# Attention followed by a gated MLP on one core: the third group's softmax denominators summed on GpSimd in float32

## The chip, the cores and the metric

One core of a Trainium2 chip runs the whole program. The metric is the device time of one execution in microseconds (us), the median of several runs; lower is better. The engines are named as in the profile: PE (TensorE, the matmul array; PEld is its weight load), DVE (VectorE), ACT (ScalarE), POOL (GpSimd) and SP (SyncE, which issues transfers here).

## What is computed

Eight batches, twelve heads, 448 tokens, head dimension 64. Queries and keys are normalised by their root mean square, attention is taken in each head, and its output goes, token by token, through a layer of 768 to 2048 with a leaky gate and a layer back to 768.

```python
def rmsnorm(x, g):
    rms = np.sqrt(np.mean(x * x, axis=-1, keepdims=True) + 1e-06)
    return x / rms * g
q_n, k_n = (rmsnorm(q, g_q), rmsnorm(k, g_k))
scores = np.matmul(q_n, k_n.transpose(0, 1, 3, 2)) / np.sqrt(64)
scores = scores - np.max(scores, axis=-1, keepdims=True)
attn = np.exp(scores)
attn = attn / (np.sum(attn, axis=-1, keepdims=True) + 1e-09)
x = np.matmul(attn, v)        # then heads side by side: 3584 x 768
h = x @ w_in                  # 768 -> 2048
g = np.maximum(h, 0.0) + alpha * np.minimum(h, 0.0)
out = g @ w_out               # 2048 -> 768
```

The denominators of the softmax, `np.sum(attn)` over the keys, are what the change is about. The kernel uses a fixed bias in the exponential in place of the maximum.

## The kernel before

**Tiles.** A batch has three *groups* of four heads; `y` counts groups over all batches, 0 to 23, so y = 2, 5, 8, ... is the third group of a batch. The 128 partitions hold two heads at a time (g = 0 and 1, 64 partitions each), and `par` = 0 and 1 are the other two. The 448 keys are cut into J = 7 chunks of 64.

**Attention of a group.** `score(y, j)` makes the scores of one chunk of keys against all queries in PSUM (tile sc, L323); `soft(y, j)` takes the exponential on ACT (L337) into `expT[y][:, j]`, 128 partitions by 2 x 448 in float16, with the keys of the chunk on the partitions. `den(ys)` sums over keys by products with a tile of ones, so that the denominators come out repeated over partitions (tile dn, L352 by way of `over_keys`); `attv(ys, half)` does the same walk with the values as weights (tiles av and avb). `over_keys` has 28 or 56 small products for a group: m = 64 columns of weights up to group 8, m = 32 from group 9 on (EARLY = 9), 64 rows each, so that four or eight of them use separate parts of the array. The loop over chunks j is the outermost, and each part accumulates over j. `log` (L369) and `invert` (L374) make 1/denominator on ACT as exp(-ln d), and a product on DVE (L403, L401) writes the normalised output into `xT`.

The first two groups of a batch are treated as a pair: one `den` for both. The third group stands alone, with a `den` of its own.

**MLP.** `up(b, ft)` is a *gate group*: six products of 128x448 into one PSUM bank (hT or hTa, L418), the scaled copy ah on ACT (L458), the maximum on DVE (L462) into gT. `down(b0, t, oh)` is a *down group*: sixteen products of 128x384 (op or opa, L472), a copy on DVE (L484), and two stores issued on SP.

**PSUM.** Pool pss has two buffers of two banks for scores. Pool psf has two single banks with tag "mm", shared by the gate groups hT, the down groups op, and avb. Pool psa has one buffer of two banks with tag "acc": dn and av, and now and then a gate or down group, then called hTa or opa (the flag `spare`).

**Normalisation of q and k.** For each group: load (SP), square on POOL (L152), sum on DVE (L160), root on ACT (L170, L171), scaling on POOL (L176), transposition by a transfer from group 7 on, the gain on DVE (L285).

**Order.** All engines' queues are written out by hand in program order; nothing reorders them. The unit is the *burst* n, 69 in all: two to four scores and exponentials, with a `den` or an `attv` between them where `dens[n]` or `avs[n]` says so, and behind them `gaps[n]`, a list of gate and down groups of an earlier batch. A planner fills the gaps: `cost(n)` estimates a burst's own TensorE time, UP = 1.13 and DOWN = 2.6 that of the groups, and each burst gets work until its share of the period is spent. `prep`, `post`, `roots` and `jobs` hang the loads, squares, roots and sums of later groups on bursts, counted back from `den_at` and `av_at`. In the last part, after burst 68, `rest` holds the last batch's MLP.

For a third group, the `den` stands in one burst and the `attv` in the next, each between scores:

```python
if n in dens and not lead:
    den(dens[n])
if n in avs and not lead:
    for half in (1, 0) if avs[n] == (0, 1) else (0,):
        attv(avs[n], half)
```

Of the kernel before, what the change touches and what calls it, by code (L numbers as in the profile page):

```python
# [21 lines left out]
def kernel(  # L22
# [26 lines left out]
    TD = min(7, NG)  # L49
    EB = 3  # L50
    EARLY = 3 * G
    assert G == 3

    cst = ctx.enter_context(tc.tile_pool(name="cst", bufs=1))
# [19 lines left out]
    nc.vector.memset(epsb, RMS_EPS)  # L74
    ones = cst.tile([128, 64], FP16, name="ones", tag="ones")
    nc.vector.memset(ones, 1.0)
    ident = cst.tile([128, 128], FP16, name="ident", tag="ident")
    make_identity(nc, ident)
    ident32 = cst.tile([32, 32], FP32, name="ident32", tag="ident32")
# [233 lines left out]

    expT, rden, scs = {}, {}, {}

    def score(y, j):
        qT, kT = qkT[y, "q"], qkT[y, "k"]
        sc = pss.tile([128, 2, 512], FP32, name="sc", tag="sc")
        m = 64 if y < EARLY else 32
        for c in range(64 // m):  # L320
            for par in range(2):
                for g in range(2):
                    nc.tensor.matmul(  # L323
                        out=sc[ds(64 * g + m * c, m), par, :S].rearrange(
                            "p (j c) -> p j c", j=J
                        ),
                        lhsT=kT[ds(64 * par, 64), j, g, ts(c, m)],
                        rhs=qT[ds(64 * par, 64), :, g, :],
                        start=True,
                        stop=True,  # L330
                    )
        scs[y, j] = sc

    def soft(y, j):
# [4 lines left out]
            scale=QK_SCALE, bias=expb[:, 0:1],  # L339
        )  # L340

    def over_keys(accs, ys, weights):

        m = 64 if len(ys) == 1 and ys[0] < EARLY else 32
        if len(ys) == 2:
            heads = [(y, par, 0) for y in ys for par in range(2)]
        else:
            heads = [(ys[0], par, c) for par in range(2) for c in range(64 // m)]
        for j in range(J):
            for h, (y, par, c) in enumerate(heads):  # L350
                for g in range(2):
                    nc.tensor.matmul(  # L352
                        out=accs[g][ds(m * h, m), :S],
                        lhsT=weights(g, y, par, ts(c, m), j),
                        rhs=expT[y][ds(64 * g, 64), j, par, :],
                        start=(j == 0),
                        stop=(j == J - 1),
                    )

    def den(ys):  # L360
        dn = psa.tile([128, 2, 512], FP32, name="dn", tag="acc")
        over_keys(
            (dn[:, 0], dn[:, 1]), ys, lambda g, y, par, c, j: ones[ds(64 * g, 64), c]
        )
        rden[ys] = dn

    def log(ys):
        r = att.tile([128, 2, S], FP32, name="rden", tag="rden")
# [146 lines left out]
    m = 0  # L515
    while m < NG * J or steps:
        n = len(bursts)
        while steps:
            ys, values = steps[0]
            if values:  # L520

                if n in dens and ys != (G - 1,):
                    break
                avs[n] = ys
                av_at.update((y, n) for y in ys)
            else:
                if n in avs or any(last_in.get(y, n) >= n for y in ys):
                    break
                dens[n] = ys
                den_at.update((y, n) for y in ys)  # L530
            steps.pop(0)
        both = len(avs.get(n, ())) == 2
        late = both or n in dens and n in avs or any(
            y >= G for y in dens.get(n, avs.get(n, ()))
        )
        limit = 2 + late + (both and avs[n][0] >= G)
        bursts.append([])
        while len(bursts[n]) < limit and m < NG * J:
            y, j = divmod(m, J)
            if j == 0 and y >= EB and av_at.get(y - EB, n) == n:  # L540

                if y - EB not in av_at or both and len(bursts[n]) < 3:
                    break
                split[n] = min(len(bursts[n]), 2)
            bursts[n].append((y, j))
            first_in.setdefault(y, n)
            if j == J - 1:
                last_in[y] = n
            m += 1
# [3 lines left out]
    def at(n, f, *a):  # L553
        prep.setdefault(max(int(n), 0), []).append((f, a))

    def after(n, f, *a):
        post.setdefault(max(int(n), 0), []).append((f, a))
# [3 lines left out]
        for y in range(1, NG)  # L561
    }
    turn_at[2], turn_at[G] = 5, av_at[0]
    turn_at.update((y, den_at[y - 2]) for y in range(TD, NG) if y % G == 1)
    turns = {n: y for y, n in turn_at.items()}
    jobs = {}
    for y in range(G, NG):

        early = y < G + 2
        if early:  # L570
            n = turn_at[y - 1] + 1
        elif y == G + 2:
            n = den_at[G - 1]
        elif y == 2 * G:
            n = turn_at[y] - 4
        elif y % G == 1:
            n = den_at[y - 4] - 1
        elif y % G:
            n = den_at[y - G]
        else:  # L580
            n = av_at[y - 4]
        if y in (3 * G - 1, 3 * G):

            after(den_at[G] - (y < 3 * G), load_qk, y)
        else:
            at(n - (6 if early else 3 if y == 2 * G else 4 if y < 3 * G else 5), load_qk, y)
        for nm in "qk":
            if y != 2 * G:
                after(n - 2, square, y, nm)
            if early:  # L590
                after(n, reduce, y, nm, (0, 1) if (y, nm) == (G, "k") else None)
            else:
                jobs.setdefault(n + (y == G + 2 and nm == "k"), []).append((reduce, (y, nm)))
        if y == 3 * G:
            after(n, *jobs[n].pop()[:1], y, "k")
        roots[n + 1 + (y in (G + 2, 3 * G))] = y
# [20 lines left out]
    def cost(n):  # L617
        return (
            0.31 + 0.19 * len(bursts[n])
            + 1.35 * ((n in dens) + len(avs.get(n, ()))) + (0.9 if turns.get(n, TD) < TD else 0.0)  # L620
        )

    def wide(n):
# [4 lines left out]
    for b in range(B - 1):  # L628
        lo, hi = av_at[G * b + G - 1], av_at[G * b + 2 * G - 1]
        ups, old, new = (list(u) for u in periods[b])  # L630
        mlp = sum(u[0] for u in ups + old + new)
        stop = hi
        if b == 0:

            stop -= len(new)
        per = (mlp + sum(cost(n) for n in range(lo, stop))) / (stop - lo)
        clock = 0.0
        for n in range(lo, hi):
            clock += cost(n)
            free = True  # L640
            while ups or old or new:
                if old and (not ups or free and (
                    wide(n) or len(old) > sum(wide(c) for c in range(n, hi))
                )):
                    u = old.pop(0)
                elif ups:
                    u = ups.pop(0)
                else:
                    u = new.pop(0)
                gaps[n].append(u[1:])  # L650
                clock += u[0]
                free = False
                ahead = 0.5 * (UP if ups else DOWN)
                if not (ups or old) and n + len(new) < hi:
                    break
                if b == 0:
                    goal = 5 + round((NF - 5) * (n - lo) / (stop - 1 - lo))
                    if NF - len(ups) >= goal and n < stop - 1:
                        break
                    continue  # L660
                short = n in turns and len(gaps[n]) < 2
                if n < hi - 1 and not short and clock + ahead > per * (n - lo + 1):
                    break
# [78 lines left out]
    for n in range(NB):  # L742
# [33 lines left out]
        for t in tiles[:1] if wait else tiles[1:2] if lead else first_tiles:  # L776
# [3 lines left out]
                    scale(mid[n], nm)  # L780
                follow(mid[n], "k")
            soft(*t)
        if n in dens and not lead:
            den(dens[n])
        if n in avs and not lead:

            for half in (1, 0) if avs[n] == (0, 1) else (0,):
                attv(avs[n], half)
# [11 lines left out]
        if n in roots:  # L800
# [11 lines left out]
                    f(*a)  # L812
            if y >= TD:
                turn_dma(y)
        if n in dens and not lead:
            log(dens[n])
            if gaps[n] and gaps[n][0][0] is down:
                invert(dens[n])
            else:
                late = [(1, invert, (dens[n],))]  # L820
# [2 lines left out]
        spare_at, clock = [], 0.0  # L823
        taken = n + 1 in dens or n + 1 in avs or turns.get(n + 1, TD) < TD
        for k, (f, a) in enumerate(gaps[n]):
            free = 2.3 if n in dens else (0.1, 1.2, 0.0)[len(avs.get(n, ()))]
            since += 1
            if clock >= free and not turns.get(n, TD) < TD and (
                since > 2 and not (taken and k == len(gaps[n]) - 1) or free == 0.0 and k == 0
# [13 lines left out]
        for k, (f, a) in enumerate(gaps[n]):  # L843
# [3 lines left out]
            else:  # L847
                f(*a, spare)
                done += 1
                if n in jobs and not (lead and done < 5):  # L850
                    g, c = jobs[n].pop(0)
                    g(*c)
                    if not jobs[n]:
                        del jobs[n]
# [8 lines left out]
            g(*c)  # L863
        if n in (0, 1, 4):
            spin(1)
        for f, a in jobs.pop(n, []) + post.get(n, []):
            f(*a)
    for k, (f, a) in enumerate(rest):
# [31 lines left out]
```

## Time and profile before

| | |
|---|---|
| three runs | 429.08, 428.44, 429.0 us |
| median | 429.0 us |
| span of the profiled execution, first to last instruction | 426.9 us |
| TensorE clock granted, mean | 0.998 |
| idle time of PE put down to a wait for ACT's exponentials, whole span | 2.2 us |
| busy in 203.8 to 252.9 us, one batch period (49.1 us) | PE 48.95, ACT 33.6, DVE 23.5, POOL 21.3 us |

The page lists the span of the execution that was profiled, not a time around it; the runs' times lie about 2 us above the span. Records of matmuls overlap at their ends, as the array is pipelined, so a group's price on TensorE is read from the start of one group to the start of the next, not from its duration. A name such as "out<-in" gives the tile written and those read; "64*32 64x448" means 64 rows of weights by 32 columns, and 448 columns streamed through.

### The profile page before, as it was taken

The numbers are of one execution on the slowest core, as the hardware profiler recorded it, in microseconds if no ns is written. First come the engines' busy times: TensorE is split into PE (matmuls) and PEld (weight loads), VectorE is DVE, ScalarE is ACT, GpSimd is POOL, SyncE is SP. The second block draws the span as 40 slices with busy tenths as digits, with TensorE's granted clock in tenths as the row PEclk, the third lists the DMA queues.
The fourth block names the chain that finished last, engine by engine and source line by source line (L and its number), as shares of the span: only waits on it lengthen the run. The fifth ranks groups of instructions, "written<-read, shape, count | busy, mean of one in ns | idle before, by whom it ended". The sixth has DMA issues, their size and how long they took to land.

```text
span 426.9 us, 11531 instructions
## 1 busy us (share of the span) xinstructions
PE 414.8 (97%) x4975; PEld 216.8 (51%) x4975; DVE 209.4 (49%) x318; ACT 276.2 (65%) x384; POOL 172.1 (40%) x137
## 2 busy tenths in 40 slices
PE   7889999999999999999999999999999999999995
PEld 3344454544455455544555555554555445555564
DVE  4875964556454455446255453635443453243321
ACT  5898887778875685767675685778575676133200
POOL 6789993574558019360556209370343000000000
PEclk9999999999999999999999999999999999999999
DMA  8999999999288804975377814973183201211033
GB/s 184 233 246 225 212 199 216 234 174 215 43 167 148 210 3 83 201 172 113 63 129 172 206 40 82 189 129 84 34 151 72 49 1 22 57 38 37 20 75 76
DMA packets 68532, 53.40 MB, mean 125 GB/s; under 512 B 35568, under 2 KB 68480, under 8 KB 68480
## 3 DMA queue, kind: packets, MB, share of 16 engines
q1 hardware_dynamic: 53680, 39.73, 42.5%
q0 software_dynamic: 13984, 11.81, 18.5%
q10 hardware_dynamic: 816, 1.11, 1.1%
q8 instruction: 39, 0.64, 0.6%
q14 instruction: 13, 0.11, 0.1%
HBM read 45.62 MB, written 11.01 MB: 133 GB/s over the span
## 4 chain that ended last, share of the span: by engine, by line
PE 90%; ACT 4%; POOL 2%; DVE 2%; issue 1%; ACTq 1%; POOLq 0%
PE op L472 29%; PE hT L418 22%; PE hTa L418 11%; PE sc L323 8%; PE opa L472 6%; PE dn L352 5%; PE av L352 5%; PE avb L352 2%; ACT expT L337 2%; POOL sq L152 1%; DVE osb L484 1%; ACTq L105 1%; PE tps L299 1%; PE hTb L418 1%; DVE ss L160 0%
## 5 line engine op out<-in xcount | busy, mean ns | idle before, releaser
L337 ACT ACTIVATE expT<-sc,expb 128x896 f16<-128x896 f32 x168 | 161.3, 1004 | 35.7 <-PE sc L323 34.9
L472 PE MATMUL op<-w_out_sb,gT 128*128 128x384 f16 (+1 forms) x752 | 126.3, 323 | 0.0
L176 POOL TENSOR_TENSOR qs<-nat,rr 128x896 f16<-128x896 f32 x41 | 69.2, 1710 | 138.9 <-issue 92.6
L472 PEld LDWEIGHTS <-gT 128*128 128x128 f16 x912 | 85.8, 98 | 64.6 <-issue 12.0
L418 PEld LDWEIGHTS <-w_in_sb 128*128 128x128 f16 x768 | 73.2, 98 | 72.4 <-issue 7.7
L418 PE MATMUL hT<-xT,w_in_sb 128*128 128x448 f16 x510 | 106.6, 353 | 0.0
L458 ACT ACTIVATE ah<-hT,cols 128x448 f16<-128x448 f32 x84 | 53.1, 634 | 45.0 <-PE hT L418 44.8
L152 POOL TENSOR_TENSOR sq<-nat 128x896 f32<-128x896 f32 (+1 forms) x47 | 75.0, 1618 | 7.6 <-DMA nat<-in_q_dram 7.5
L462 DVE TENSOR_TENSOR gT<-hT,ah 128x448 f16<-128x448 f32 x85 | 52.8, 623 | 47.5 <-ACT ah L458 47.3
L484 DVE COPY osb<-op 128x384 f32<-128x384 f32 (+1 forms) x47 | 25.8, 548 | 87.9 <-PE op L472 87.9
L323 PE MATMUL sc<-qT,kT 64*32 64x448 f16 (+1 forms) x1092 | 53.4, 356 | 4.5 <-ACT expT L337 2.2
L418 PE MATMUL hTa<-xT,w_in_sb 128*128 128x448 f16 x246 | 53.2, 352 | 0.0
L160 DVE TENSOR_REDUCE ss<-sq 128x14 f32<-128x896 f32 (+1 forms) x48 | 48.8, 1039 | 1.0 <-POOL sq L152 0.8
L458 ACT ACTIVATE ah<-hTa,cols 128x448 f16<-128x448 f32 x41 | 26.0, 635 | 31.3 <-PE hTa L418 31.3
L462 DVE TENSOR_TENSOR gT<-hTa,ah 128x448 f16<-128x448 f32 x41 | 25.6, 624 | 26.3 <-ACT ah L458 26.3
L323 PEld LDWEIGHTS <-kT 64*32 64x32 f16 (+1 forms) x1092 | 15.5, 93 | 35.5 <-issue 28.4
L472 PE MATMUL opa<-w_out_sb,gT 128*128 128x384 f16 x160 | 27.7, 326 | 0.0
L403 DVE TENSOR_TENSOR xT<-av,rden 128x896 f16<-128x896 f32 x16 | 17.5, 1091 | 20.1 <-PE av L352 15.6
L352 PEld LDWEIGHTS <-vt 64*32 64x32 f16 (+1 forms) x1260 | 19.0, 94 | 13.1 <-issue 2.1
L352 PE MATMUL dn<-expT,ones 64*32 64x448 f16 (+1 forms) x812 | 24.2, 350 | 0.9
L352 PE MATMUL av<-expT,vt 64*32 64x448 f16 (+1 forms) x812 | 24.1, 349 | 0.0
L369 ACT ACTIVATE rden<-dn 128x896 f32<-128x896 f32 x16 | 14.5, 908 | 7.3 <-PE dn L352 7.3
(60 smaller groups left out, 167.0 us busy)
## 6 DMA issues: line engine op xcount, KB each, us to landing
out_dram<-osb SPq DMA_DIRECT2D x109, 96.0 KB, 2.5
nat<-in_q_dram SPq DMA_DIRECT2D x46, 224.0 KB, 5.1
nat<-in_k_dram SPq DMA_DIRECT2D x46, 224.0 KB, 5.8
vt<-in_v_dram POOLq DMA_DIRECT2D x16, 336.0 KB, 7.6
w_in_sb<-in_moe_w_in_dram POOLq DMA_DIRECT2D x12, 256.0 KB, 8.4
w_out_sb<-in_moe_w_out_dram POOLq DMA_DIRECT2D x4, 768.0 KB, 10.5
nat<-in_q_dram ACTq DMA_DIRECT2D x2, 224.0 KB, 4.5
nat<-in_k_dram ACTq DMA_DIRECT2D x2, 224.0 KB, 6.2
```

What stands on the lines that cost most here:

```text
L152: nc.gpsimd.tensor_mul(out=sqf[:, c], in0=src[:, c], in1=src[:, c])
L160: nc.vector.tensor_reduce(out=o[:, c], in_=sqs[y, nm][:, c], axis=AXIS_X, op=ALU.add)
L176: eng.tensor_mul(out=t.rearrange("p j h d -> p h j d"), in0=nat[y, nm], in1=rr_t[y][:, "qk".index(nm)].unsqueeze(3).broadcast_to((128, 2, ...
L323: nc.tensor.matmul(out=sc[ds(64 * g + m * c, m), par, :S].rearrange("p (j c) -> p j c", j=J), lhsT=kT[ds(64 * par, 64), j, g, ts(c, m)], r ...
L337: nc.scalar.activation(out=expT[y][:, j], in_=scs[y, j][:, :, :S], func=AF.Exp, scale=QK_SCALE, bias=expb[:, 0:1],)
L352: nc.tensor.matmul(out=accs[g][ds(m * h, m), :S], lhsT=weights(g, y, par, ts(c, m), j), rhs=expT[y][ds(64 * g, 64), j, par, :], start=(j = ...
L403: nc.vector.tensor_mul(out=x, in0=av[:, :, :S], in1=r)
L418: nc.tensor.matmul(out=hT[:, :S], lhsT=w_in_sb[:, g * G + i, ts(ft, 128)], rhs=xT[b][:, g, i, :], start=(i == 0 and g == 0), stop=(i == G ...
L458: nc.scalar.activation(out=ah, in_=hT[:, :S], func=AF.Copy, scale=alpha_sb[:, ft : ft + 1])
L462: nc.vector.tensor_max(out=gT[:, ft, ds((b & 1) * S, S)], in0=hT[:, :S], in1=ah)
L472: nc.tensor.matmul(out=ops[c][:, :PW], lhsT=gT[:, ft, ts(t, 128)], rhs=w_out_sb[:, ft, ds(oh * OH + c * PW, PW)], start=(ft == 0), stop=(f ...
L484: nc.vector.tensor_copy(out=o[:, ts(c, PW)], in_=ops[c][:, :PW])
```

## The change

For the third groups from batch 2 on (y = 8, 11, 14, 17, 20, 23; `pre`), the product of ones with seven chunks goes. In its place:

- `add_up`: after each burst, GpSimd adds the exponentials of the burst's chunks to a float32 tile `rden[y,]`, six additions of 128 x 896 for a group.
- `den_pre`: in the burst of the values, ahead of them, products of float32 ones with that sum, once (four for y = 8, eight from y = 11 on), into two banks of "mm"; DVE copies them to SBUF over the sum.
- `log_pre` and `invert` follow behind the values' products, on ACT.

The `den` burst of such a group is gone. The values can't come in the same burst as the last chunk's exponentials or the next one, only from the second burst after (`last_in + pre`), and the burst takes up to four scores. The planner's price of such a burst is 0.4 for the denominators, where a `den` has 1.35. Loads, squares and turns of some later groups are moved one burst earlier. The rest of the diff keeps the planner's and the gaps' rules in step.

```diff
+    PRE = 3 * G - 1
...
+    ones32 = cst.tile([128, 64], FP32, name="ones32", tag="ones32")
+    nc.vector.memset(ones32, 1.0)
...
+    def pre(ys):
+        return len(ys) == 1 and ys[0] >= PRE and ys[0] % G == G - 1
...
+    def add_up(y, j):
+
+        if j == 0:
+            return
+        e = expT[y]
+        if j == 1:
+            rden[y,] = att.tile([128, 2, S], FP32, name="rden", tag="rden")
+        s = rden[y,]
+        nc.gpsimd.tensor_add(out=s, in0=e[:, 0] if j == 1 else s, in1=e[:, j])
...
+    def den_pre(ys):
+        y = ys[0]
+        m = 64 if y < EARLY else 32
+        accs = [psf.tile([128, 512], FP32, name="dnb", tag="mm") for _ in range(2)]
+        for h in range(128 // m):
+            for g in range(2):
+                nc.tensor.matmul(
+                    out=accs[g][ds(m * h, m), :S],
+                    lhsT=ones32[ds(64 * g, 64), :m],
+                    rhs=rden[ys][ds(64 * g, 64), h * m // 64, :],
+                    start=True,
+                    stop=True,
+                )
+        for g in range(2):
+            nc.vector.tensor_copy(out=rden[ys][:, g], in_=accs[g][:, :S])
+
+    def log_pre(ys):
+        r = rden[ys]
+        nc.scalar.activation(out=r, in_=r, func=AF.Ln)
...
-                if n in dens and ys != (G - 1,):
+                if n in dens and ys != (G - 1,) and not pre(ys):
                     break
...
-                if n in avs or any(last_in.get(y, n) >= n for y in ys):
+                if n in avs or any(last_in.get(y, n) + pre(ys) >= n for y in ys):
                     break
...
-        limit = 2 + late + (both and avs[n][0] >= G)
+        limit = 2 + late + (both and avs[n][0] >= G) + pre(dens.get(n, ()))
...
-    turn_at.update((y, den_at[y - 2]) for y in range(TD, NG) if y % G == 1)
+    turn_at.update(
+        (y, den_at[y - 2] - pre((y - 2,))) for y in range(TD, NG) if y % G == 1
+    )
...
-            n = den_at[y - 4] - 1
+            n = den_at[y - 4] - 1 - pre((y - 2,))
...
-            n = den_at[y - G]
+            n = den_at[y - G] - pre((y - G,))
...
-                after(n - 2, square, y, nm)
+                after(n - 2 - (y % G == G - 1 and pre((y - G,))), square, y, nm)
...
-            + 1.35 * ((n in dens) + len(avs.get(n, ()))) + (0.9 if turns.get(n, TD) < TD else 0.0)
+            + (0 if n not in dens else 0.4 if pre(dens[n]) else 1.35)
+            + 1.35 * len(avs.get(n, ())) + (0.9 if turns.get(n, TD) < TD else 0.0)
...
-        if n in dens and not lead:
+        sums = n in dens and pre(dens[n])
+        if sums:
+            den_pre(dens[n])
+            attv(avs[n], 0, False, (log_pre, invert))
+        elif n in dens and not lead:
             den(dens[n])
-        if n in avs and not lead:
+        if n in avs and not lead and not sums:
...
+        for y, j in tiles:
+            if pre((y,)):
+                add_up(y, j)
         for f, a in jobs.pop(n, []) + post.get(n, []):
             f(*a)
```

More of the change, by code (lines that the diff above doesn't have):

```diff
@@ L585 @@
         else:
-            at(n - (6 if early else 3 if y == 2 * G else 4 if y < 3 * G else 5), load_qk, y)
+            at(n - (6 if early or y % G == G - 1 and pre((y - G,)) else 3 if y == 2 * G else 4 if y < 3 * G else 5), load_qk, y)
         for nm in "qk":
             if y != 2 * G:
-                after(n - 2, square, y, nm)
+                after(n - 2 - (y % G == G - 1 and pre((y - G,))), square, y, nm)
             if early:
@@ L641 @@
             while ups or old or new:
-                if old and (not ups or free and (
+                two = n in dens and pre(dens[n]) and len(gaps[n]) < 2
+                if old and (not ups or (free or two) and (
                     wide(n) or len(old) > sum(wide(c) for c in range(n, hi))
@@ L814 @@
                 turn_dma(y)
-        if n in dens and not lead:
+        if n in dens and not lead and not sums:
             log(dens[n])
@@ L825 @@
         for k, (f, a) in enumerate(gaps[n]):
-            free = 2.3 if n in dens else (0.1, 1.2, 0.0)[len(avs.get(n, ()))]
+            free = 2.9 if sums else 2.3 if n in dens else (0.1, 1.2, 0.0)[len(avs.get(n, ()))]
             since += 1
@@ L849 @@
                 done += 1
-                if n in jobs and not (lead and done < 5):
+                if n in jobs and not (lead and done < 5) and (
+                    n < av_at[2 * G - 1] or done % 2
+                ):
                     g, c = jobs[n].pop(0)
```

## The prediction

> **What bounds the kernel now.** I read the page's busy times and the chain that ended last first, then TensorE's timeline through one batch, then the rows of the operations that the change takes away or adds.
>
> ```profile
> PE 414.8 (97%) x4975; PEld 216.8 (51%) x4975; DVE 209.4 (49%) x318; ACT 276.2 (65%) x384; POOL 172.1 (40%) x137
> ...
> PE 90%; ACT 4%; POOL 2%; DVE 2%; issue 1%; ACTq 1%; POOLq 0%
> ```
>
> TensorE is busy for 414.8 of 426.9 us and holds 90% of the chain: whatever lengthens its queue lengthens the kernel. A batch in the middle shows how tightly (TensorE alone; start, duration, records; the time from one start to the next is what a group costs, because the ends overlap):
>
> ```profile
> 214.62 2.77 PE L472 MATMUL opa<-w_out_sb,gT 128*128 128x384 f16 x16
> 217.32 0.57 PE L323 MATMUL sc<-qT,kT 64*32 64x448 f16 x16
> 218.04 1.52 PE L352 MATMUL dn<-expT,ones 64*32 64x448 f16 x56
> 219.36 0.39 PE L323 MATMUL sc<-qT,kT 64*32 64x448 f16 x8
> 219.68 2.77 PE L472 MATMUL op<-w_out_sb,gT 128*128 128x384 f16 x16
> 222.38 0.57 PE L323 MATMUL sc<-qT,kT 64*32 64x448 f16 x16
> 222.77 1.51 PE L352 MATMUL av<-expT,vt 64*32 64x448 f16 x56
> 224.10 0.37 PE L323 MATMUL sc<-qT,kT 64*32 64x448 f16 x8
> 224.40 2.77 PE L472 MATMUL op<-w_out_sb,gT 128*128 128x384 f16 x16
> 227.01 1.30 PE L418 MATMUL hTa<-xT,w_in_sb 128*128 128x448 f16 x6
> ```
>
> The third group's denominators (dn at 218.04) cost 219.36 - 218.04 = 1.32 us for 56 products. Each product uses a 64x32 part of the array and eight parts run at once, so this is seven waves of 0.187 us, the price of one pass of 448 columns. Ahead of dn, two scores take 218.04 - 217.32 = 0.72 us where the same two take 0.39 at 222.38: 0.33 us of waiting, for opa's accumulator to be copied out. Leaving the whole-array shape for a part costs 0.09 us (op to sc 2.70, op to hTa 2.61), going back about 0.12.
>
> **What the change takes away.** Six denominators (y = 8, 11, 14, 17, 20, 23): 308 products, 6 x 1.32 = 7.9 us, all on the path. With them go the waits for opa's copy: 0.33 at four of them and 0.21 at the first, 1.5 us. The changed program's instruction order has 140 changes between whole-array and part products instead of 142: one round trip, 0.2 us.
>
> **What it adds on TensorE** are float32 products: eight for each of y = 11 to 23 (parts of 64x32) and four for y = 8 (64x64). The only float32 products of this trace are the warming ones at the start:
>
> ```profile
> 11.60 1.02 PE L501 MATMUL spin<-gT 128*128 128x448 f32 x2
> 12.45 0.39 PE L227 MATMUL tps<-ident,qs 128*128 128x128 f16 x4
> ```
>
> One instruction shows as two records, and the next group starts 12.45 - 11.60 = 0.85 us later. The line's shortest, middle and longest records (ns), float16 first:
>
> ```profile
> L501 PE MATMUL spin<-gT,ident x20: 352/353/581, 4.7 to 22.5; 128*128 128x448 f16 x20
> L501 PE MATMUL spin<-gT x12: 539/643/1116, 1.5 to 20.7; 128*128 128x448 f32 x12
> ```
>
> A float16 record of 352 ns is a pass of 187 and 165 to leave the array; 539 - 165 = 374 ns, so a float32 pass holds the array twice as long. A product is two passes, 0.75 us, and 0.1 at its first weights makes the 0.85. No row shows such products side by side on parts of the array, so the price has two ends: 0.75 to 0.85 us when all eight run at once, and 8 x 0.75 = 6.0 us when each waits for the one ahead (3.0 for y = 8).
>
> I take a value between, from what the rows do show. Records start in the program's order, and products in float16 run together only because neighbours in the queue use different parts. Here the two passes of one product use the same part, so the second cannot start before 0.374 us, and the next product, behind it, cannot start sooner either. It then starts beside that second pass. Eight products make a staircase of nine steps, 9 x 0.374 = 3.37 us. The values' products begin beside the last step (-0.19), the first weights add 0.1: 3.28 us, against 1.32 removed. For y = 8 five steps: 1.87 - 0.19 + 0.1 = 1.78. Sum: 5 x 3.28 + 1.78 = 18.2 us added for 7.9 removed, **+10.3 us**. If every step pays 0.1 for weights, it is about 3.9 for each and +13.5; with 3.1 and no weights exposed, +9.2.
>
> [...] No run here shows the two passes next to other parts.
>
> **What else moves on TensorE.** The accumulators of a gate group are free about 1.49 us after the next group starts: hTa ends near 233.63, its ACT pass runs 233.83 to 234.47, its maximum 234.49 to 235.12. The pool "mm" has two buffers and the accumulator "acc" is the third. The planner now deals more groups to "mm": in the changed order two places have three gate groups in a row there, and two have two followed by a down group. The third arrives 1.13 us after the second's start and waits 0.36, or a little more when an exponential is ahead on ACT: 4 x 0.4 = **+1.5 us** (ends: 0, when other waits cover it, and 3).
>
> The second product wants the "mm" buffer of the down group just finished: its copy (0.56 us, L484) ends some 0.82 us after the group's last issue, two scores cover 0.48. The 0.34 us left lie under the first product's own first pass of 0.374; without a staircase they would be open.
>
> **GpSimd's sums**, 36 adds of 128x896. Nearest rows:
>
> ```profile
> L176 POOL TENSOR_TENSOR qs<-nat,rr 128x896 f16<-128x896 f32 x41 | 69.2, 1710 | 138.9 <-issue 92.6
> ...
> L152 POOL TENSOR_TENSOR sq<-nat 128x896 f32<-128x896 f32 (+1 forms) x47 | 75.0, 1618 | 7.6 <-DMA nat<-in_q_dram 7.5
> ```
>
> At 1.7 us they add 61 us to an engine busy 172, 10.2 us in each batch, where its timeline shows one idle stretch of 18.9 us. Place: in the batch of y = 17 the first add can start near 206.1, when the second exponential is out. Six adds end at 216.3. Exponentials of y = 17 are out by about 213, so GpSimd is the later one. TensorE reaches the products near 221.9: the order puts av, avb, opa, two gate groups and a down group between. Cover: 5.6 us, gone when an add costs over (221.9 - 206.1) / 6 = 2.6 us. Bounds for an add: nothing below, and above twice the row, 3.4 us, which is the third rival. Behind the adds in GpSimd's queue stand the squares of the next group and the load of v. The squares end near 219.7, ahead of their sums on DVE in the burst of the products; the loads of q and k on SP were put one burst earlier to match, and wait for scalings as before. Cost taken: nothing.
>
> [...]
>
> **DVE, ACT.** Two copies of 128x448 out of PSUM a group (0.62 each by L401's row), 7.5 us on an engine at 49%. The chain behind a group's products is copies 1.25, logarithm 0.9, exponential 0.95, product 1.09 = 4.2 us. It lies beside the rest of the values (1.3), two scores (0.4) and two down groups (5.3), which use "mm" and not "acc". At the end, where y = 23 stands alone, one down group and four products of the first gate group give 1.1 + 2.6 + 0.75 after the staircase: 4.5, enough. Cost: 0 to 0.5.
>
> **Sum.** +10.3 - 1.5 - 0.2 + 1.5 = +10.1 us, made on the profiled span of 426.9 and so 437.0 there; the median of the runs, 429.0, lies 2.1 above that span, so I add it there: **439**.
>
> **The rivals.** (1) All parts run at once: a sum costs 0.75 plus the 0.34 us for the second buffer, 1.1 for 1.32; 6 x -0.2 - 1.5 - 0.2 + 1.5 = -1.5, 427.5; without the buffer waits 6 x -0.57 - 1.7 = -5.1, 424. For it: float16 parts do overlap eightfold here. Against: the two passes of a product never do. It decides when the queue may pass a held second pass. (2) Float32 products never share the array: 5 x (6.0 - 1.32) + (3.0 - 1.32) = +25, 454. For it: every float32 row here is whole-array and alone; against: parts are separate for float16. (3) The sums come late: adds of 3.4 us end at 226.5, 4.6 us late, six times: +28, about 465 with the staircase. Against: both rows and the idle stretch. That the change isn't carried out is excluded: the changed order has the 44 float32 products and 36 adds.
>
> **How the numbers follow.** Staircase 0.75 (436 to 444 by its bounds), rival 1 0.18, rival 2 0.05, rival 3 0.02. 0.2%, 0.9 us, is about what a measurement of this kernel can tell from no change. Rival 1 lies mostly below 428.1 and has a little within: faster 0.16, same 0.04, slower 0.80. The range reaches from the staircase down into rival 1, 427.5, and up to 446; below lies about 0.10, above 0.07.
>
> **What would show it.** About 3.1 us from the first float32 record to the first of the values', in steps of 0.37, is the staircase; all starts within 0.1 us is rival 1; 0.75 apart rival 2. TensorE waiting for GpSimd ahead of them is rival 3. Waits of 0.4 us for DVE in rows of three gate groups test the buffers. I am wrong if the products' group takes less than 1.4 us.

## The result and the profile after

The changed kernel takes 427.2 us (median of five, 427.17 to 427.42) where the kernel before, measured beside it, takes 428.61. The ratio is 0.996, with a 95% interval of 0.9947 to 0.9972: faster by 1.4 us. The forecast was 439.0, slower; its own first rival, "all parts run at once", had 427.5. The span of the profiled execution went from 426.9 to 425.6 us.

The page of the changed kernel, busy times and the chain by engine:

```profile
PE 413.7 (97%) x4755; PEld 216.5 (51%) x4755; DVE 222.4 (52%) x331; ACT 275.3 (65%) x384; POOL 239.4 (56%) x173
...
PE 86%; ACT 5%; DVE 4%; POOL 2%; issue 1%; ACTq 1%; POOLq 0%
```

TensorE's busy time fell by only 1.1 us though it has 220 records fewer (308 gone, 88 new), and the chain now passes through DVE for 4%: something was saved and something else came in. GpSimd took the 67 us of additions without becoming the bound.

TensorE itself gained less than the span did. The last lines of its timeline, of the kernel before and of the changed one:

```profile
416.91 5.40 PE L472 MATMUL op<-w_out_sb,gT 128*128 128x384 f16 x48
...
416.40 5.40 PE L508 MATMUL op<-w_out_sb,gT 128*128 128x384 f16 x48
```

Its last matmul ends at 422.31 us before and at 421.80 after, 0.5 us earlier. The rest of the span's 1.3 us lies behind it: the last two stores land 2.8 and 3.0 us after their issue in the kernel before, and 1.9 and 2.1 us in the changed kernel and in every variant below. The change does not touch these stores; why they took longer in the kernel before was not tested.

TensorE's timeline of the changed kernel through the same place of the batch as was shown before (start, duration, name, records):

```profile
215.37 5.37 PE L508 MATMUL op<-w_out_sb,gT 128*128 128x384 f16 x32
220.67 0.57 PE L329 MATMUL sc<-qT,kT 64*32 64x448 f16 x16
221.06 1.29 PE L389 MATMUL dnb<-rden,ones 64*32 64x448 f32 x13
221.81 0.35 PE L368 MATMUL av<-expT,vt 64*32 64x448 f16 x1
221.82 0.55 PE L389 MATMUL dnb<-rden,ones 64*32 64x448 f32 x3
222.00 1.51 PE L368 MATMUL av<-expT,vt 64*32 64x448 f16 x48
...
224.00 5.21 PE L508 MATMUL op<-w_out_sb,gT 128*128 128x384 f16 x31
```

The float32 products start at 221.06 and the first of the values' at 221.81: 0.75 us, where the staircase had 3.1. The wait of 0.33 us for opa's copy is gone, as forecast: the two scores ahead of the products take 221.06 - 220.67 = 0.39 us. The starts of the sixteen passes of another group (y = 11), read off the trace in us from the first one, show how the 0.75 comes about:

```text
0.00  0.33 0.34 0.34 0.35 0.36 0.37 0.38 0.38  0.73 0.74 0.74 0.75 0.76 0.77 0.78
```

One pass at 0.00, then, within 0.05 us, the seven other first passes and the first product's second pass, then the seven second passes. The trace does not name the parts. With the estimate of 0.374 us for a pass (539 - 165 ns), none of the records at 0.33 to 0.37 can be the first part's second pass, which so starts at 0.376, behind the first passes of parts that stand later in the program. What the seven waited for until 0.33 is the second bank of "mm", as the weight loads of the same moment show:

```profile
172.27 0.30 PEld L389 LDWEIGHTS dnb<-rden,ones 64*32 64x32 f32 x2
172.46 1.29 PE L389 MATMUL dnb<-rden,ones 64*32 64x448 f32 x13
...
172.79 0.15 PEld L389 LDWEIGHTS dnb<-rden,ones 64*32 64x32 f32 x11 [0.22 <-DVE osb L520]
```

The first product's two weights load at 172.27; the others wait for DVE's copy of the down group (osb). Only four of the eight products write the second bank; the other three of the seven start with them, between 0.33 and 0.376, and stand behind the second product in the program. So in this group a wait of 0.33 us for a bank kept back the products behind it, where the first part's second pass, not started until 0.376, did not. The forecast had this wait, 0.34 us, and had it lie under the first product's own first pass. With all parts at once it does not: the second passes of the late seven start at 0.73 to 0.78, beside the values. From the first float32 pass to the down group behind it are 224.00 - 221.06 = 2.94 us; the experiment "The down group out of the way", without that wait, has 2.57. So a group's denominators cost 0.75 + 0.37 = 1.12 us on the path, against 1.32.

This holds for y = 11, 14, 17 and 20. For y = 23 no scores stand between the down group and the products, and the passes behind the first product wait 0.72 us for the second bank. From the products to the next down group are 369.63 - 366.67 = 2.96 us, of which the values take 1.45, as in the kernel before (370.14 - 368.69). That leaves 1.5 us where the float16 products had 365.98 - 364.53 = 1.45: no gain. For y = 8 the same reckoning gives 1.0.

### The profile page after: what moved, and what is told of

Its sections match the earlier page's. It is cut to its first block, busy times and chain, and to the rows that moved or that the text cites. A ratio compares the mean times of both kernels' runs of the same rounds, so it can differ in the third digit from the quotient of the medians.

```text
span 425.6 us, 11138 instructions
## 1 busy us (share of the span) xinstructions
PE 413.7 (97%) x4755; PEld 216.5 (51%) x4755; DVE 222.4 (52%) x331; ACT 275.3 (65%) x384; POOL 239.4 (56%) x173
## 4 chain that ended last, share of the span: by engine, by line
PE 86%; ACT 5%; DVE 4%; POOL 2%; issue 1%; ACTq 1%; POOLq 0%
PE op L508 29%; PE hT L454 21%; PE hTa L454 9%; PE sc L329 8%; PE opa L508 6%; PE av L368 5%; PE dn L368 3%; ACT expT L343 2%; PE avb L368 2%; PE dnb L389 2%; ACT ah L494 2%; DVE gT L498 1%; POOL sq L155 1%; DVE ss L163 1%; ACTq L108 1%
## 5 line engine op out<-in xcount | busy, mean ns | idle before, releaser
L454 PE MATMUL hT<-xT,w_in_sb 128*128 128x448 f16 x552 | 114.7, 353 | 0.8 <-DVE gT L498 0.5
L494 ACT ACTIVATE ah<-hT,cols 128x448 f16<-128x448 f32 x91 | 57.4, 632 | 46.5 <-PE hT L454 45.6
L498 DVE TENSOR_TENSOR gT<-hT,ah 128x448 f16<-128x448 f32 x92 | 57.3, 623 | 50.7 <-ACT ah L494 49.8
L356 POOL TENSOR_TENSOR rden<-rden,expT 128x896 f32<-128x896 f32 x30 | 56.8, 1895 | 2.4
L454 PE MATMUL hTa<-xT,w_in_sb 128*128 128x448 f16 x204 | 44.1, 352 | 0.0
L494 ACT ACTIVATE ah<-hTa,cols 128x448 f16<-128x448 f32 x34 | 21.6, 634 | 21.0 <-PE hTa L454 20.9
L498 DVE TENSOR_TENSOR gT<-hTa,ah 128x448 f16<-128x448 f32 x34 | 21.2, 624 | 19.6 <-ACT ah L494 18.9
L368 PEld LDWEIGHTS <-vt 64*32 64x32 f16 (+1 forms) x1260 | 21.4, 94 | 12.7 <-issue 2.5
L368 PE MATMUL av<-expT,vt 64*32 64x448 f16 (+1 forms) x812 | 26.6, 349 | 0.0
L356 POOL TENSOR_TENSOR rden<-expT 128x896 f32<-128x896 f16 x6 | 11.3, 1878 | 20.9 <-ACT expT L343 20.9
```

Of the source, the lines that this page charges most:

```text
L356: nc.gpsimd.tensor_add(out=s, in0=e[:, 0] if j == 1 else s, in1=e[:, j])
L368: nc.tensor.matmul(out=accs[g][ds(m * h, m), :S], lhsT=weights(g, y, par, ts(c, m), j), rhs=expT[y][ds(64 * g, 64), j, par, :], start=(j = ...
L454: nc.tensor.matmul(out=hT[:, :S], lhsT=w_in_sb[:, g * G + i, ts(ft, 128)], rhs=xT[b][:, g, i, :], start=(i == 0 and g == 0), stop=(i == G ...
L494: nc.scalar.activation(out=ah, in_=hT[:, :S], func=AF.Copy, scale=alpha_sb[:, ft : ft + 1])
L498: nc.vector.tensor_max(out=gT[:, ft, ds((b & 1) * S, S)], in0=hT[:, :S], in1=ah)
```

## The experiments

Where no range stands behind a time, it is that of one execution.

**Three passes held behind the first.** Each float32 product is issued twice in a row on its part.

```diff
         for h in range(128 // m):
-            for g in range(2):
+            for g in (0, 0, 1, 1):
```

> Each float32 product of ones is issued twice in a row on the same part of the array (16 instead of 8 for y = 11 to 23, 8 instead of 4 for y = 8), so three passes stand held behind the first, ahead of the next part's products. Theory P (a held pass holds only its own part): a part has four passes, 4 x 0.374 = 1.5 us instead of 0.75, all parts side by side; +0.75 us for each of six groups, +4.5 us on the changed kernel's 427.2, 431.7. Theory S (products start in program order, a staircase): each part but the last adds three steps, 25 x 0.374 = 9.4 us instead of 0.75, 13 x 0.374 = 4.9 for y = 8; about +47 us, 474. A mixed theory L (the queue can pass one held pass and no more): steps of 0.75 us for each part, about 6 us, +27 us, 454.

Measured: 432.7 us, 1.0 above P's 431.7 and nothing like S or L. The 32 passes of y = 11 start in rounds 0.37 us apart, and the values' products 1.5 us after the first one:

```profile
173.33 2.03 PE L389 MATMUL dnb<-rden,ones 64*32 64x448 f32 x27
174.83 0.35 PE L368 MATMUL av<-expT,vt 64*32 64x448 f16 x1
```

Four passes in a row on one part held no other part back. The staircase is excluded. The 1.0 us over P is spread over the groups: from the first pass to the down group are 3.84 us where the changed kernel has 2.94, so a group costs 0.9 us more and not 0.75.

**Seven float16 products in a row on a part.** In one denominator of a pair the loop over chunks is made the innermost.

```diff
-        for j in range(J):
-            for h, (y, par, c) in enumerate(heads):
-                for g in range(2):
+        at = [(j, h, g) for j in range(J) for h in range(len(heads)) for g in range(2)]
+        if inside:
+            at.sort(key=lambda x: x[1:])
...
+            inside=ys == (12, 13),
```

> In one float16 denominator of a pair (y = 12 and 13) the seven chunks j become the innermost loop: seven products in a row on one part of the array, then the next part. Theory P: the eight parts still run side by side, 7 x 0.187 = 1.3 us as before, time unchanged at 427.2. Theory S: eight parts with six steps each and one wave, 49 x 0.187 = 9.2 us, +7.8 us, 435.0. Theory L (a limited look past held products): between them, the starts in the trace say how many.

Measured: 431.4 us, neither P nor S. On TensorE's timeline the 56 products, which in the changed kernel take 1.32 us, run from 203.14 to 208.55 and later:

```profile
203.14 5.00 PE L370 MATMUL dn<-expT,ones 64*32 64x448 f16 x53
207.79 0.52 PE L329 MATMUL sc<-qT,kT 64*32 64x448 f16 x7
207.98 0.73 PE L370 MATMUL dn<-expT,ones 64*32 64x448 f16 x3
```

The starts go 0.00, 0.19, 0.38, 0.57, 0.57, 0.76, 0.77, 0.95, 0.96, 1.13, 1.15, 1.16. Read with 0.19 us a pass, the second part begins at 0.57, when the first part's fourth product starts and its last three have not; the third begins at 1.15. Seven parts at 0.57 each and the last one at 1.31 add up to 5.3 us, against some 5.4 in the trace. From these starts the author estimated that parts step from the fifth pass in a row on; the change issues two.

**Blocks of four and of five.** To test that estimate, two other denominators get their chunks in blocks of four and of five.

```diff
+        at.sort(key=lambda x: (x[0] // block, x[1:], x[0]))
...
+            block={(12, 13): 4, (15, 16): 5}.get(ys, 1),
```

> The changed kernel with the chunks of two float16 denominators dealt in blocks: four chunks in a row on a part for the pair (12, 13), five in a row for (15, 16), the rest of the seven in a second round. Theory Q (each part has a queue of its own: one product running and three waiting behind it; a fifth holds everything behind it): (12, 13) costs 1.32 us as before, all parts side by side; (15, 16) pays one step of 0.19 us for each part, starts of new parts 0.19 us apart, about 7 x 0.19 + 7 x 0.19 = 2.6 us or a little less, +1.2 us on 427.2, 428.4. Theory S (program order over all parts): blocks of four give 8 x 3 steps and more, over 5 us; blocks of five over 6 us; +10 us together, 437. Theory T (one common window of held products, about six, whatever the part): both blocks show steps, the block of four as well.

The timeline around the two, block of four first:

```profile
204.15 1.67 PE L369 MATMUL dn<-expT,ones 64*32 64x448 f16 x50
...
206.10 0.66 PE L510 MATMUL op<-w_out_sb,gT 128*128 128x384 f16 x3
...
253.99 2.36 PE L369 MATMUL dn<-expT,ones 64*32 64x448 f16 x50
...
257.04 0.66 PE L510 MATMUL op<-w_out_sb,gT 128*128 128x384 f16 x3
```

From the first product to the down group behind the next score: 1.95 us with four, 3.05 with five, and 1.63 in the changed kernel. With four in a row six parts start within 0.06 us; with five a new part starts every 0.19 us. Those are the starts of theory Q and of neither S nor T, under which the block of four would step as well. Two things of the block of four are not in Q: two parts start only some 0.2 us after the first, and the 24 products of the second round start one by one, about 0.03 us apart, which loses 0.3 us. Why stays open. The time, 430.15, is 1.7 us more than Q had, but 1.0 of it is lost ahead of anything edited: the granted clock was 0.83 between 10 and 20 us, and the products of y = 8 start at 123.85 where the changed kernel has 122.85. So the rows are used and not the time.

**Six float32 passes on a part.** The same for float32: each product three times in a row.

```diff
-            for g in range(2):
+            for g in (0, 0, 0, 1, 1, 1):
```

> Each float32 product of ones issued three times in a row, six passes on a part (24 products, 48 passes for y = 11 to 23; 12 and 24 for y = 8). Theory Q (one pass running, three waiting, in each part): the fifth and sixth pass of a part hold the queue for two steps, so parts start 0.75 us apart: 7 x 0.75 + 6 x 0.374 = 7.5 us instead of 0.75 for the five, 3 x 0.75 + 2.2 = 4.5 for y = 8; about +37 us, 465. Theory P (no limit for float32 passes): 6 x 0.374 = 2.2 us, +9 us, 436.

Measured: 463.5 us, Q's 465 and not P's 436. In the group of y = 11 the passes start two or three at a time, 0.38 us apart, and the last one at 7.35 us; the forecast of Q was 7.5 to the end, that of P 2.2. So the steps came with six float32 passes in a row on a part as well, where four, in the first experiment, had rounds 0.37 us apart.

**GpSimd's sum undone alone.** Everything of the change stays but the additions; the products are float16 over seven chunks again, in the same burst and banks.

```diff
...
-                    lhsT=ones32[ds(64 * g, 64), :m],
-                    rhs=rden[ys][ds(64 * g, 64), h * m // 64, :],
...
+        over_keys(accs, ys, lambda g, y, par, c, j: ones[ds(64 * g, 64), c])
+        rden[ys] = att.tile([128, 2, S], FP32, name="rden", tag="rden")
...
-        for y, j in tiles:
-            if pre((y,)):
-                add_up(y, j)
```

> Undoes one part: GpSimd's sums are gone, and the products in the values' burst are float16 ones over all seven chunks again (56 or 28), into the same two banks, with the same copies, logarithm and planning. Theory 1 (the float32 products gain, the new plan costs): 1.32 us for 0.75, and the 0.33 us for the second bank stays open ahead of them; +0.55 us for each of six groups, +3.3, 430.5, slower than the kernel before. Theory 2 (the gain comes from merging the bursts and dropping the wait for opa, the sums are worth little): 427.2 or less. Theory 3 (GpSimd's adds hold up DVE, through memory or their order): taking them away gives something back, below 429.

Measured: 430.4 us (430.35 to 430.51), ratio to the kernel before 1.004 (1.0026 to 1.0054). Theory 1 had 430.5. The new plan by itself is a loss of about 1.7 us by the times, and of 2.6 on TensorE, whose last matmul ends at 424.87 us here and at 422.31 before (the last stores give the rest back); the sum on GpSimd, with two float32 passes on a part in place of seven float16 ones, wins 3.2. Busy GpSimd time falls from 188 to 122 us between 60 and 360 us, and nothing is given back for it, so theory 3 falls.

**The down group out of the way.** In the burst ahead of the float32 products of y = 11, 14, 17 and 20 the last group goes to "acc".

```diff
+        nxt = pre(dens.get(n + 1, ()))
...
-            if clock >= free and not turns.get(n, TD) < TD and (
+            if nxt and k == len(gaps[n]) - 1 and since > 1 or clock >= free and not turns.get(n, TD) < TD and (
```

> The changed kernel, and the last gate or down group of the burst ahead of the float32 products goes to the accumulator acc where that has been free for a group (y = 11, 14, 17, 20), so that both banks of mm are free for the products. Theory 1 (the second product waits 0.33 us for the bank of the down group just finished, and in two batches that down group waits 0.41 us as third in mm): 4 x 0.33 + 2 x 0.41 = 2.1 us less, 425.1. Theory 2 (the wait moves to the values, which need acc, behind the copy of the down group): the products cover 0.75 of the 0.82 us, but if the copy comes later the gain is under 0.5 us, 426.7 or more.

Measured: 425.1 us (424.87 to 425.97), ratio to the kernel before 0.9922 (0.9909 to 0.9934): theory 1 to the tenth. The timeline of this version at the place shown above:

```profile
217.16 2.76 PE L508 MATMUL opa<-w_out_sb,gT 128*128 128x384 f16 x16
219.86 0.57 PE L329 MATMUL sc<-qT,kT 64*32 64x448 f16 x16
220.24 0.94 PE L389 MATMUL dnb<-rden,ones 64*32 64x448 f32 x16
221.00 1.51 PE L368 MATMUL av<-expT,vt 64*32 64x448 f16 x56
222.32 0.56 PE L329 MATMUL sc<-qT,kT 64*32 64x448 f16 x16
222.81 2.45 PE L508 MATMUL op<-w_out_sb,gT 128*128 128x384 f16 x14
```

All sixteen passes are through together, and the down group follows 2.57 us after the first. The values do not wait for "acc": they start at 221.00, 0.76 us after the first, and the float32 products cover the copy.

**Three gate groups in a row.** On top of that, in bursts of five gate groups the third goes to "acc" instead of the second.

```diff
+        five = taken and [f for f, _ in gaps[n]] == [up] * 5
...
-            if nxt and k == len(gaps[n]) - 1 and since > 1 or clock >= free and not turns.get(n, TD) < TD and (
+            if k == 2 if five else nxt and k == len(gaps[n]) - 1 and since > 1 or clock >= free and not turns.get(n, TD) < TD and (
```

> The version of e4, and in bursts of five gate groups the third instead of the second goes to acc, so that three in a row no longer share the two banks of mm (twice in the program). Theory 1 (each third group waits 0.41 us for its bank): 0.8 us less than e4's 425.1, 424.3. Theory 2 (what holds the third is DVE's order, its sums of squares ahead of the maximum, and not the bank): no gain, 425.1.

Measured: 424.2 us (424.09 to 424.34), ratio 0.9885 (0.9869 to 0.9902), 0.9 us better than the version before it, as theory 1 had it. The row that it removes, from the changed kernel, and the same burst without it:

```profile
248.39 2.43 PE L454 MATMUL hT<-xT,w_in_sb 128*128 128x448 f16 x12
251.07 1.29 PE L454 MATMUL hT<-xT,w_in_sb 128*128 128x448 f16 x6 [0.25 <-DVE gT L498]
252.29 0.57 PE L329 MATMUL sc<-qT,kT 64*32 64x448 f16 x16
```

```profile
246.62 1.30 PE L454 MATMUL hTa<-xT,w_in_sb 128*128 128x448 f16 x6
247.75 2.43 PE L454 MATMUL hT<-xT,w_in_sb 128*128 128x448 f16 x12
250.12 0.57 PE L329 MATMUL sc<-qT,kT 64*32 64x448 f16 x16
```

Two groups take 251.07 - 248.39 = 2.68 us while the third waits for its bank, and 2.37 with the change to the scores when it doesn't. This version is the fastest measured here.

**GpSimd's cover.** The first of the six additions is done three times over, so the sums come 3.9 us later.

```diff
-        nc.gpsimd.tensor_add(out=s, in0=e[:, 0] if j == 1 else s, in1=e[:, j])
+        for _ in range(3 if j == 1 else 1):
+            nc.gpsimd.tensor_add(out=s, in0=e[:, 0] if j == 1 else s, in1=e[:, j])
```

> The changed kernel, and the first of GpSimd's six adds of each group is done three times over (the same result), two adds of 1.96 us more, 3.9 us. In the changed kernel the sums end 4.0 to 4.7 us ahead of the products that read them for y = 11 to 23, but only 0.1 us ahead for y = 8. Theory 1 (the sums are hidden by that cover and nothing else): the five pay nothing or 0.1, y = 8 pays 3.8; 431.0. Theory 2 (GpSimd's queue is also behind: the squares after the adds are late and hold DVE): more than 432. Theory 3 (the adds start earlier or run beside others): 427.2.

Measured: 433.5 us, 2.5 more than theory 1. TensorE's waits of this kernel have one for GpSimd, exactly as large as forecast:

```profile
PE dnb L390 <- POOL rden L357: 3.8, 1, 3.8
```

For the five other groups TensorE's products show no idle time; their cover shrank to between 0.05 and 0.74 us. The other 2.3 us of the span are not theory 2 either: from y = 11 on the products of every group stand 6.1 us later than in the changed kernel, and no group adds to that. They are lost behind the wait, where the next down group comes 5.19 us after the first product and not 2.96. The granted clock was 0.50 and 0.73 there: the windows around the wait, with TensorE's granted clock in the column behind the five engines' busy times, and the products of y = 8 (shortest, middle and longest record in ns) here and in the changed kernel:

```profile
122.00:126.50 4.50, 0.73 (x18) 0.14 (x16) 2.49 (x2) 1.91 (x2) 4.34 (x4) 0.87 0.20 44
126.50:130.00 3.50, 3.46 (x32) 1.51 (x36) 1.16 (x2) 0.34 (x1) 3.50 (x3) 0.50 0.02 5
130.00:134.00 4.00, 4.00 (x41) 1.65 (x34) 2.38 (x3) 3.80 (x6) 1.12 (x3) 0.73 0.75 108
...
L390 PE MATMUL dnb<-rden,ones x8: 951/976/1002, 126.5 to 127.4; 64*64 64x448 f32 x8
...
L389 PE MATMUL dnb<-rden,ones x8: 536/562/587, 122.9 to 123.5; 64*64 64x448 f32 x8
```

After 3.8 us without matmuls the clock was 0.50 for 3.5 us and 0.73 in the next 4. An estimate from these two windows, half of the first and 0.27 of the second lost, is 1.75 + 1.1 = 2.8 us at most, which holds the 2.3. That the wait brought the clock down is not shown: this is one execution, and the run with the blocks has a low clock, 0.83 between 10 and 20 us, where nothing was edited.

## Why the prediction was wrong, step by step

**The step that failed** is the price of the float32 products: "the second cannot start before 0.374 us, and the next product, behind it, cannot start sooner either". The first half is right, by the trace's 0.376. The second is wrong: eight products take 0.75 us side by side, and no run shows the staircase of 3.37. That records start in the program's order agreed with the rows of the trace before (the 56 products of a denominator on 64x32 parts come in eights, each within 0.04 us and 0.19 behind the one before), but none of them had two passes in a row on one part beside products on other parts, so none tested it. In the changed kernel first passes start from 0.33 us on, ahead of a second pass at 0.376. The sum had 18.2 us for the six groups; the runs show 4 x 1.12, 1.5 for y = 23 and 1.0 for y = 8, 7.0 us. The prediction's own sign of being wrong, a group of products under 1.4 us, came for all but y = 23. The two ends of the price, 0.75 and 6.0, were right to be kept; the value between was drawn from an order that no row had tested for such products.

**Right, with sizes.** The denominators gone, 7.9 us; the waits for opa's copy gone, 1.5 us, seen as 0.39 us of scores. The new waits of gate and down groups for "mm": forecast 4 x 0.4 = 1.5 (it is 1.6); the trace has four of 0.41, two of 0.21 where DVE's sums of squares stand ahead of a maximum, and one of 0.24 ahead of the denominators at 106.93, which wait for a gate group's maximum: 2.3 us. The experiments on the down group and on three gate groups took the four away. The wait for the second bank: 0.34 us forecast, 0.33 seen, with the condition under which it shows.

**GpSimd.** An addition takes 1.89 us (1.96 from one start to the next), not the 1.7 of the nearest rows; the sums of y = 17 run from 205.29 to 217.02 and are read at 221.06, so the cover is 4.0 us and not 5.6. It was enough for five groups. For y = 8 it was 0.1 us, which the working for one batch did not show: that group's additions stood behind squares and could not start before 110.97.

**The sum as it should have been**, for TensorE: -7.9 + 7.0 - 1.5 - 0.2 + 2.3, and -0.25 for y = 8, whose denominators on 64x64 parts took 120.85 - 119.40 = 1.45 us and 0.12 ahead of them for the change of shape, and not the 1.32 of the others. That is -0.55 us, and TensorE's last matmul comes 0.5 us earlier. The other 0.8 of the span's 1.3 us are the last stores, for which neither the sum nor a rival had a term.

So the first rival had the price of the float32 products right for four groups (1.1 us, measured 1.12), but that it came within 0.3 us of the time is in part luck. Its -1.5 us (its terms add up to -1.4) was some 0.9 too much for TensorE, because of y = 23 and the waits, and the stores made up for it.

## What to carry to other kernels

A price that no row shows deserves both ends as real cases; the value between should not be given most of the weight because of an order that no row has tested. With TensorE busy for 97% of the span, replacing seven float16 passes of 0.19 us by two float32 ones of 0.37 saved no more than 1.4 us, as the new order brought waits for banks: these were worth 3.0 us (427.2 to 424.2), over twice the change's own gain. Part of a small gain can lie behind TensorE's last matmul, here 0.8 of the span's 1.3 us, so compare where TensorE ends before explaining all of it. And in the one execution with a wait of 3.8 us on TensorE, 2.3 us more were lost behind that wait.

## What the runs showed of the hardware

- In the changed kernel (y = 11) six float32 passes on 64x32 parts started at 0.33 to 0.37 us, ahead of the second pass of the first product, which by the estimate of 0.374 us for a pass is a record at 0.376 and stands ahead of them in the program.
- With four float16 passes in a row on a part six of the eight parts started within 0.06 us, two some 0.2 us later; with four float32 ones the passes of a group started in rounds 0.37 us apart and the values' products 1.5 us after the first. With five float16 ones a new part started every 0.19 us; with seven the second started at 0.57 and the third at 1.15, and the 56 products took 5.4 us instead of 1.32; with six float32 ones the last of 48 passes started at 7.35 us.
- In the groups of y = 11, 14, 17 and 20 the second float32 product waited for its PSUM bank until 0.33 us behind the first, and the products behind it, also those for the other bank, did not start sooner; at y = 23 the passes behind the first product started from 0.72 us on.
- A float32 product of 448 columns leaves two records. On a 64x32 part the second starts 0.376 us after the first, where the whole-array rows gave an estimate of 0.374; behind a group's eight products the first of the values' starts after 0.75 us, and without the wait for the bank after 0.76.
- GpSimd's additions of 128x896 into float32 took 1.88 us where they read float16 alone and 1.89 where they read the float32 sum as well; its multiplications of that size took 1.68 to 1.71 in the kernel before.
- In one execution, the granted clock was 0.50 in the 3.5 us that followed 3.8 us without matmuls in the middle of the kernel, and the span grew by 2.3 us more than the wait.
